# Polysketch attention and a rational activation on one Trainium2 core: two coefficients of the activation joined by accumulating transfers

## The chip, the cores and the metric

The kernel runs on one core of one Trainium2 chip. The metric is the device time of one execution in microseconds (us). Three executions of the kernel before took 264.3, 264.67 and 264.9 us; the median is 264.67 us.

## The reference, cut to what matters

Attention with a sketched polynomial feature map gives 4352 tokens of 128 features. They pass through a two-layer network whose activation is a quotient of two polynomials with coefficients a[0..3] and b[0..1]:

```python
h = x @ w_in                       # 4352 x 128 times 128 x 2048
P = a[0] + a[1] * h + a[2] * h**2 + a[3] * h**3
Q = 1.0 + abs(b[0]) * abs(h) + abs(b[1]) * h**2
g = P / (Q + 1e-06)
return g @ w_out                   # 2048 x 128
```

The attention in front of it builds, for each of 4 batches, products of two sketches (8 x 8 = 64 features for each head), sums k-features times v over the sequence, and divides numerator by denominator for each token.

## The kernel before, in words

**Units.** The network is cut into 21 units (`UNITS`): a stretch of tokens (mostly 512) and a group of 128-wide slices of the 2048 hidden features (mostly 8). A full unit is a tile of 128 x 4096 bf16 values. Units 3 to 16 are full ones, in pairs that share their tokens; units 0 to 2 and 17 to 20 are smaller. For a full unit these steps run:

- `H` (`hidden`, L498): TensorE multiplies, in four parts of 1024 columns, into PSUM.
- `E` (`evac`, L504): ScalarE copies each part to `hh` in bf16.
- `U` (`d_abs`, L511): VectorE clears the sign bit, u = |h|.
- `W` (`d_w`, L519): VectorE makes w = |b1| u + |b0|. `Y` (`d_y`, L524): VectorE multiplies w by u, so that w is Q - 1.
- `L` and `X` (`a_ln` L547, `a_exp` L551): ScalarE takes r = exp(-ln(1 + 1e-6 + w)) in two halves of 2048 columns; this is 1/Q.
- `P` (`p`): g = a3 h + a2 in two halves, each on VectorE (`.d`, L529) or on ScalarE (`.a`, L532). `V` (`d_hp`, L542): VectorE multiplies g by h.
- `S` (`d_s`, L555): s = h r. `G` (`d_g`, L559): g = g s. Both are on VectorE.
- `Or`, `Os`, `Og` (`gather`, L571): TensorE adds up r, s and g against w_out scaled by a0, by a1 and by 1. `ST` (L588) turns the finished 512 tokens round, `OUT` stores them.

Units named in `TWO` leave the a1 term out of `Os`: a step `A` (`plus`, L538) has the GpSimd queue issue two transfers per unit that add a DRAM tensor of a1 values (`ones`, f32) onto g between `V` and `G`. Then g = (a3 h^2 + a2 h + a1) s, and the eight matmuls of `Os` fall away. Before, units 6, 9 and 12 do so.

**What sets the order.** Nothing is scheduled by the compiler: `ORDER` is a list written out in full, and each engine works through its own instructions in that order. `H6.2` is part 2 of step H of unit 6; `K` and `Q` steps are the attention of a batch's keys and of a cut of its queries, `F` and `I` loads, `Z` matmuls on an idle tile. Semaphores follow from the tiles that a step reads and writes. Pools set how far steps may run ahead: `u` has one buffer, `w` two, `g` four, `hh` three, `r` and `s` two. GpSimd's queue holds only the transfers of `A` once the set-up is over. SP's queue holds all loads, the attention's writes and repeated reads through DRAM (`dw`, `dr`), and the stores.

Of the kernel before, what the change touches and what calls it, by code (L numbers as in the profile page):

```python
# [35 lines left out]
I0 I11 I1 I2 K0.T0 SS0 Z10 K0.s0 K0.T1 K0.c0.a K0.T2 K0.f0 Q0.0.T Z2 K0.s1 Z2 Q0.0.sk I3 Z2 K0.p0 I8 F1.k I7 I9 I5
I4 I10 I6 K0.c1.a K0.f1 Q0.0.c.d Q0.0.f Q0.1.T K0.p1 K0.k1.d Q0.2.T K1.T0 K0.k0.a Q0.1.sk K1.T1 Q0.0.p Q0.2.sk
Q0.0.pl.a Q0.1.c.a Q0.2.c.a Q0.0.r K1.T2 Q0.0.x K1.s0 Q0.0.b K1.s1 K1.c0.a Q0.0.kk.a w4.a K1.c1.a AB0 w0.a Q0.3.T
w2.d K1.f0 Q0.1.f K1.f1 w5.d H0.0 E0.0 Q0.1.p Q0.3.sk H1.0 H2.0 Q0.1.pl.a w1.a w3.a E1.0 Q0.3.c.a U0.0 Q0.1.r W0.0
P0.0.d Y0.0 V0.0 Q0.1.x Q0.2.dw F1.q U1.0 Q1.0.T W1.0 Q1.1.T P1.0.d Y1.0 H2.1 Q1.0.sk L0.0 E2.0 X0.0 E2.1 Q1.0.c.a  # L40
Q1.2.T S0.0 V1.0 U2.0 G0.0 P2.0.a F1.v K1.p0 K1.p1 Q0.1.b Or0.0 Os0.0 Og0.0 K1.k1.a K1.k0.a F2.k Q0.2.dr Q0.2.f
Q0.3.dw Q1.0.dw F2.q L1.0 Q0.1.kk.a Q0.2.p Q0.2.pl.a K2.T0 W2.0 K2.T1 Q0.2.r K2.T2 Q0.2.x Q1.1.sk Q1.1.c.a X1.0
K2.s0 Q0.2.b K2.s1 Q0.2.kk.a K2.c0.a Y2.0 H3.0 L2.0 K2.c1.a E3.0 S1.0 V2.0 K2.f0 G1.0 Q0.3.dr X2.0 Q1.1.dw H3.1
Q1.2.sk H3.2 E3.1 H3.3 Q1.0.dr Q2.0.T K2.f1 Q0.3.f S2.0 Q2.1.T G2.0 Q2.0.sk Q2.2.T E3.2 Q1.2.c.a E3.3 P3.0.a H4.0
Q0.3.p E4.0 Q0.3.pl.a Q2.0.c.a P3.1.a H4.1 U3.0 Q1.0.f W3.0 Q0.3.r Y3.0 Q1.0.p Q2.1.sk H4.2 Q1.0.pl.a E4.1 Q1.0.r
Q0.3.x Q1.0.x L3.0 P4.0.d V3.0 H4.3 Q0.3.b Os1.0 Q1.0.b Or1.0 Os2.0 E4.2 E4.3 F3.k Q1.1.dr Q1.1.f Q1.2.dw F3.q
Q2.1.c.a Q0.3.kk.a Q1.0.kk.a Q2.0.dw AW0 F2.v Q1.2.dr Q2.1.dw X3.0 Q2.0.dr Og1.0 H5.0 Q1.1.p Or2.0 L3.1 E5.0 X3.1
U4.0 P4.1.d W4.0 V4.0 Y4.0 H5.1 E5.1 Q1.1.pl.a H5.2 K2.p0 H5.3 S3.0 Q1.1.r P5.0.d G3.0 Q1.1.x Q3.0.T Q1.2.f L4.0
E5.2 X4.0 E5.3 K2.p1 Og2.0 ST2 U5.0 K2.k1.a K3.T0 W5.0 Q2.2.sk H6.0 K2.k0.a P5.1.a E6.0 L4.1 H6.1 Or3.0 Or3.1
Q1.1.b Q2.2.c.a E6.1 X4.1 Q1.1.kk.a Q3.0.sk H6.2 H6.3 Q1.2.p V5.0 Y5.0 L5.0 S4.0 P6.0.d Q2.0.f G4.0 Q2.1.dr E6.2  # L50
H7.0 X5.0 E6.3 L5.1 Q2.0.p Q2.0.pl.a Q1.2.pl.a Or4.1 H7.1 Or4.0 U6.0 Q3.1.T Q2.0.r Q1.2.r K3.T1 W6.0 K3.T2 Q2.1.f
E7.0 X5.1 P6.1.a Q2.2.dw E7.1 Q3.0.c.a Q3.0.dw OUT2 Y6.0 V6.0 Q2.0.x Os3.0 Og4.0 H7.2 L6.0 Q2.2.dr A6.0 F3.v X6.0
E7.2 L6.1 H7.3 E7.3 Os4.0 Og3.0 H8.0 S5.0 Q3.2.T Q1.2.x H8.1 Q1.2.b G5.0 K3.s0 P7.0.a E8.0 X6.1 E8.1 Q1.2.kk.a
Q2.0.b H8.2 U7.0 ST4 W7.0 P7.1.d Y7.0 K3.c0.a E8.2 S6.0 P8.0.d K3.f0 L7.0 Or5.0 H8.3 E8.3 P8.1.a Q2.0.kk.a Or5.1
Q2.1.p Q2.1.pl.a K3.s1 U8.0 V7.0 Q2.1.r W8.0 Q3.0.dr Q2.2.f K3.c1.a Y8.0 K3.f1 G6.0 Og5.0 Q3.1.sk H9.0 Os5.0 H9.1
X7.0 L7.1 E9.0 Q3.1.c.a X7.1 Q2.1.x Q3.1.dw L8.0 E9.1 V8.0 S7.0 H9.2 Or6.1 Or6.0 H9.3 E9.2 X8.0 E9.3 Q2.1.b H10.0
L8.1 Q2.1.kk.a Q2.2.p Og6.0 E10.0 Q2.2.pl.a X8.1 U9.0 G7.0 Q2.2.r W9.0 ST6 P9.0.a Q2.2.x Y9.0 H10.1 K3.p0 Or7.0
H10.2 E10.1 P9.1.a Or7.1 H10.3 K3.p1 E10.2 L9.0 E10.3 S8.0 V9.0 Q3.0.f U10.0 P10.0.d Q3.2.sk H11.0 X9.0 K3.k1.a
Q3.2.c.a H11.1 E11.0 L9.1 E11.1 K3.k0.a H11.2 Os7.0 G8.0 W10.0 P10.1.d Y10.0 E11.2 X9.1 H11.3 E11.3 L10.0 Og7.0
A9.0 Q3.2.dw Q3.1.dr Or8.0 Or8.1 V10.0 S9.0 U11.0 P11.0.a Q3.0.p Q3.0.pl.a X10.0 H12.0 Q2.2.b Os8.0 H12.1 Og8.0  # L60
E12.0 L10.1 Q2.2.kk.a X10.1 E12.1 OUT4 Q3.2.dr G9.0 Q3.1.f Q3.0.r W11.0 Q3.0.x Y11.0 S10.0 ST8 P11.1.a Q3.0.b
H12.2 Q3.0.kk.a E12.2 L11.0 OUT6 P12.0.d G10.0 V11.0 H12.3 E12.3 U12.0 Or9.0 Or9.1 X11.0 H13.0 E13.0 L11.1 H13.1
Q3.1.p E13.1 Q3.1.pl.a Og9.0 H13.2 H13.3 Or10.0 Or10.1 X11.1 E13.2 Q3.2.f W12.0 P12.1.d Q3.1.r Y12.0 L12.0 E13.3
P13.0.d S11.0 Q3.1.x U13.0 G11.0 W13.0 V12.0 X12.0 H14.0 Q3.1.b Q3.1.kk.a E14.0 P13.1.a H14.1 E14.1 L12.1 H14.2
Og10.0 E14.2 X12.1 H14.3 E14.3 Os10.0 Q3.2.p Y13.0 V13.0 ST10 H15.0 Or11.0 Or11.1 OUT8 A12.0 L13.0 U14.0 S12.0
P14.0.a Q3.2.pl.a X13.0 E15.0 L13.1 P14.1.d W14.0 Og11.0 H15.1 Os11.0 H15.2 E15.1 X13.1 V14.0 Y14.0 P15.0.d S13.0
G12.0 Q3.2.r E15.2 L14.0 Or12.0 H15.3 Or12.1 E15.3 U15.0 P15.1.d W15.0 Q3.2.x X14.0 H16.0 E16.0 L14.1 H16.1 Og12.0
E16.1 ST12 Y15.0 H16.2 Or13.0 Q3.2.b H16.3 X14.1 Or13.1 Or14.1 E16.2 Q3.2.kk.a L15.0 G13.0 S14.0 E16.3 U16.0.d
G14.0 W16.0.d V15.0 Y16.0 OUT12 OUT10 H17.0 Os13.0 H17.1 X15.0 E17.0 L15.1 P16.0.a E17.1 X15.1 Og14.0 H17.2 H17.3
Or14.0 Og13.0 P16.1.d E17.2 L16.0 E17.3 S15.0 V16.0 U17.0.d P17.0.d W17.0.d H18.0 H18.1 Os14.0 X16.0 E18.0 L16.1  # L70
E18.1 X16.1 P17.1.a ST14 Y17.0 G15.0 U18.0.d L17.0 W18.0.a P18.0.d S16.0 Y18.0 G16.0 H19.0 Or15.0 Or15.1 Os15.0
Or16.1 Or16.0 Os16.0 Og15.0 Og16.0 X17.0 E19.0 L17.1 U19.0.a X17.1 V17.0 W19.0.d ST16 S17.0 L18.0 P19.0.a Or17.0
H20.0 Os17.0 Or17.1 E20.0 X18.0 Y19.0 G17.0 V18.0 S18.0 Og17.0 OUT14 OUT16 U20.0.a L19.0 X19.0 W20.0.d ST17 Y20.0
V19.0 S19.0 OUT17 G18.0 P20.0.a L20.0 G19.0 V20.0 Z4 Or18.0 X20.0 Os18.0 Or19.0 Os19.0 Og18.0 S20.0 Og19.0 Or20.0
Os20.0 G20.0 Og20.0 ST20 OUT20
"""


# [1 line left out]
def kernel(  # L80
# [440 lines left out]

    def d_y(i, k):
        c = span(i, "Y", k)
        nc.vector.tensor_mul(out=at(i, "w", *c), in0=at(i, "w", *c), in1=at(i, "u", *c))  # L524
# [172 lines left out]
```

## Time and profile before

| | |
|---|---|
| median of three executions | 264.67 us (264.3 to 264.9) |
| profiled execution | 264.51 us |
| its span, first to last instruction | 262.7 us |
| granted TensorE clock | 1.000 |
| VectorE busy | 251.7 us in 234 instructions |
| ScalarE busy | 241.1 us in 230 instructions |
| TensorE busy | 253.7 us |
| GpSimd busy | 9.6 us in 31 instructions |

The span is 1.8 us shorter than the execution's own time. A busy time is the union of an engine's instructions; instructions of one engine overlap in the records by some 0.1 us at their ends, so the pace of a row (from one start to the next) is a little under its duration. TensorE's ends are modelled, so its busy time says less than the other two.

### The profile page before, as it was taken

The page shows a single profiled execution, that of the slowest core. Times are in us where ns is not written, and L with a number is a line of the kernel's source. Part 1 is how long each engine was busy: PE and PEld are TensorE (multiplying, and loading weights), DVE is VectorE, ACT ScalarE, POOL GpSimd, SP SyncE. Part 2 cuts the span into 40 slices and gives each one's busy share as a digit, 9 for nine tenths or more (in the row PEclk, how much of TensorE's full clock was granted, in tenths as well). Part 3 has the DMA queues.
Part 4 walks back from the last instruction along what each step waited for, and adds up shares of the span by engine and source line. Part 5 has one row for each costly group of instructions (what it writes and reads, how often), then busy time and mean ns, then how long its engine had stood idle before and what let it go on. Part 6 is the DMA issues. An engine that isn't in the chain of part 4 may idle for free.

```text
span 262.7 us, 3774 instructions
## 1 busy us (share of the span) xinstructions
PE 253.7 (97%) x1445; PEld 146.8 (56%) x1445; DVE 251.7 (96%) x234; ACT 241.1 (92%) x230; POOL 9.6 (4%) x31
## 2 busy tenths in 40 slices
...
GB/s 174 277 304 266 157 209 192 279 217 148 55 14 2 20 112 177 145 71 0 0 2 117 193 164 44 0 0 9 128 26 0 66 14 0 2 40 0 40 22 20
DMA packets 31888, 24.35 MB, mean 93 GB/s; under 512 B 19072, under 2 KB 26880, under 8 KB 31872
## 3 DMA queue, kind: packets, MB, share of 16 engines
...
q0 software_dynamic: 864, 3.15, 9.7%
q8 instruction: 11, 0.18, 0.3%
...
## 4 chain that ended last, share of the span: by engine, by line
PE 66%; DVE 13%; ACT 12%; issue 5%; DMA 2%; SPq 0%; DVEq 0%
PE h_ps L498 35%; PE out_ps L571 16%; PE att_ps L413 5%; ACT r L551 4%; ACT ln L547 4%; DVE s L555 3%; PE att_ps L319 3%; DVE g L559 2%; PE att_ps L291 2%; ACT hh L504 2%; DVE g L542 2%; DVE w L524 2%; PE att_ps L354 2%; DMA k_sb<-in_k_dram 2%; PE att_ps L441 1%
## 5 line engine op out<-in xcount | busy, mean ns | idle before, releaser
L498 PE MATMUL h_ps<-xT,w_in_sb 128*128 128x512 f32 (+1 forms) x320 | 126.4, 533 | 0.0
L498 PEld LDWEIGHTS h_ps<-xT,w_in_sb 128*128 128x128 f32 x320 | 58.7, 190 | 42.8 <-issue 34.3
L504 ACT CAST hh<-h_ps 128x1024 bf16<-128x1024 f32 x68 | 71.6, 1054 | 1.5 <-PE h_ps L498 1.3
L547 ACT ACTIVATE ln<-w 128x2048 f32<-128x2048 bf16 (+1 forms) x36 | 67.6, 1877 | 0.3 <-DVE w L524 0.2
L551 ACT ACTIVATE r<-ln 128x2048 bf16<-128x2048 f32 (+1 forms) x36 | 67.6, 1878 | 0.1
L571 PEld LDWEIGHTS <-w_out 128*128 128x128 bf16 x408 | 39.7, 98 | 47.6 <-issue 14.9
L555 DVE TENSOR_TENSOR s<-hh,r 128x4096 bf16<-128x4096 bf16 (+2 forms) x21 | 39.3, 1873 | 0.5 <-ACT r L551 0.3
L542 DVE TENSOR_TENSOR g<-g,hh 128x4096 bf16<-128x4096 bf16 (+2 forms) x21 | 39.4, 1874 | 0.0
L559 DVE TENSOR_TENSOR g<-g,s 128x4096 bf16<-128x4096 bf16 (+2 forms) x21 | 39.2, 1872 | 0.0
L524 DVE TENSOR_TENSOR w<-w,u 128x4096 bf16<-128x4096 bf16 (+2 forms) x21 | 39.2, 1866 | 0.0
L532 ACT ACTIVATE g<-hh,a_sb 128x2048 bf16<-128x2048 bf16 (+1 forms) x17 | 34.7, 2040 | 0.1
L571 PE MATMUL out_ps<-r,w_out 128*128 128x512 bf16 (+1 forms) x144 | 31.6, 356 | 1.3 <-DVE out_sb L588 1.3
L571 PE MATMUL out_ps<-g,w_out 128*128 128x512 bf16 (+1 forms) x144 | 30.4, 355 | 0.0
L571 PE MATMUL out_ps<-s,w_out 128*128 128x512 bf16 (+1 forms) x120 | 24.9, 350 | 1.9 <-DVE s L555 1.9
L519 DVE TENSOR_SCALAR w<-u,b_abs 128x4096 bf16<-128x4096 bf16 (+2 forms) x20 | 22.6, 1132 | 0.0
L511 DVE TENSOR_SCALAR u<-hh 128x4096 uint16<-128x4096 uint16 (+2 forms) x19 | 20.4, 1075 | 0.1
L413 PEld LDWEIGHTS att_ps<-kvz,a_all 128*118 128x118 f32 (+2 forms) x144 | 17.1, 186 | 4.4 <-issue 3.5
L413 PE MATMUL att_ps<-kvz,a_all 128*118 128x66 f32 (+2 forms) x144 | 16.9, 266 | 0.0
L529 DVE TENSOR_SCALAR g<-hh,a_sb 128x2048 bf16<-128x2048 bf16 (+1 forms) x19 | 14.6, 767 | 0.0
L538 POOL DMA_DIRECT2D g<-ones x6 | 6.3, 1337 | 166.9 <-DVE x_tok L435 81.0
L319 PEld LDWEIGHTS att_ps<-v_sb,k_p 128*64 128x64 f32 (+1 forms) x288 | 9.0, 138 | 3.5 <-issue 3.0
L285 DVE STREAM_TRANSPOSE kT<-k_sb 128x512 f32<-128x512 f32 (+2 forms) x12 | 6.2, 529 | 3.8 <-DMA k_sb<-in_k_dram 3.8
...
## 6 DMA issues: line engine op xcount, KB each, us to landing
...
```

Source lines behind the costliest of these rows:

```text
L413: nc.tensor.matmul(self.nd[:self.tl, o:o + 2 * KW], lhsT=self.group(t, c), rhs=kvz[self.b % 2][:, c, :], start=True, stop=True)
L498: nc.tensor.matmul(t[:, (x - part * m) * tl:(x - part * m + 1) * tl], lhsT=w_in_sb[:, (f0 + x) * 128:(f0 + x + 1) * 128], rhs=xT[:, p:p + ...
L504: nc.scalar.copy(out=at(i, "hh", c, ce), in_=live[i]["h", part][:, :ce - c])
L519: nc.vector.tensor_scalar(out=at(i, "w", *c), in0=at(i, "u", *c), scalar1=ab1, scalar2=ab0, op0=AX.mult, op1=AX.add)
L524: nc.vector.tensor_mul(out=at(i, "w", *c), in0=at(i, "w", *c), in1=at(i, "u", *c))
L532: nc.scalar.activation(out=at(i, "g", *c), in_=at(i, "hh", *c), func=ACT.Identity, scale=a3, bias=a2)
L542: nc.vector.tensor_mul(out=at(i, "g", *c), in0=at(i, "g", *c), in1=at(i, "hh", *c))
L547: nc.scalar.activation(out=t[:, :ce - c], in_=at(i, "w", c, ce), func=ACT.Ln, bias=1.0 + 1e-6)
L551: nc.scalar.activation(out=at(i, "r", c, ce), in_=live[i]["ln", k][:, :ce - c], func=ACT.Exp, scale=-1.0)
L555: nc.vector.tensor_mul(out=at(i, "s", *c), in0=at(i, "hh", *c), in1=at(i, "r", *c))
L559: nc.vector.tensor_mul(out=at(i, "g", *c), in0=at(i, "g", *c), in1=at(i, "s", *c))
L571: nc.tensor.matmul(outs[t0][:, :tl], lhsT=w, rhs=z, start=first and j == 0, stop=left[t0] == 0)
```

## The change

`TWO` grows from three units to six, 4, 6, 8, 10, 12 and 14. A new list `SQ` names units 5, 7, 9, 11, 13 and 15. In these the product of step `Y` is no longer made. A new step `D` (`square`) has ScalarE write w = (sqrt(|b1|) h)^2 from `hh`, in two halves. Step `W` scales u by |b0| in place. A new step `M` (`join`) has GpSimd's queue issue two transfers that add u onto w. Then `L` goes on from w as before. sqrt(|b1|) is made once, by a logarithm and an exponential on ScalarE.

In `ORDER` most halves of `P` that ScalarE made go to VectorE: 6 instead of 17 stay on ScalarE. Some small copies and sums change their engine too, and the rest of the list is written anew, with each engine's steps shifted by some places. In the changed kernel the lines are: U L516, W L527 (in place: L522), D L532, M L538, Y L542, P L547 on VectorE and L550 on ScalarE, A L556, V L560, L L565, X L569, S L573, G L577, gather L589.

```diff
-TWO = (6, 9, 12)
+TWO = (4, 6, 8, 10, 12, 14)
+SQ = (5, 7, 9, 11, 13, 15)
...
+    root1 = consts.tile([128, 1], FP, name="root1")
+    tiny = consts.tile([128, 1], FP, name="tiny")
+    nc.gpsimd.memset(tiny, 1e-30)
...
     def d_w(i, k, eng="d"):
         c = span(i, "W", k)
+        if i in SQ:
+            nc.vector.tensor_scalar(out=at(i, "u", *c), in0=at(i, "u", *c), scalar1=ab0, scalar2=None, op0=AX.mult)
+            return
...
+    def square(i, k):
+        c = span(i, "D", k)
+        nc.scalar.activation(out=at(i, "w", *c), in_=at(i, "hh", *c), func=ACT.Square, scale=root1)
+
+    def join(i, k):
+
+        c = span(i, "Y", k)
+        for x in range(c[0], c[1], 2048):
+            nc.gpsimd.dma_start(out=at(i, "w", x, x + 2048), in_=at(i, "u", x, x + 2048), accum_op=AX.add)
...
         nc.scalar.activation(out=b_abs, in_=b_sb, func=ACT.Abs)
+        if SQ:
+            nc.scalar.activation(out=root1, in_=ab1, func=ACT.Ln, bias=tiny)
+            nc.scalar.activation(out=root1, in_=root1, func=ACT.Exp, scale=0.5)
```

The part of the new list around the last `SQ` unit, which the prediction speaks of, is this (line breaks set here):

```
H14.2 Or11.0 Or11.1 H14.3 E14.2 X12.1 A12.0 S12.0 E14.3 L13.0 H15.0 Q3.2.p P14.1.d U14.0 V14.0 W14.0 E15.0 X13.0
H15.1 Os11.0 Or12.1 H15.2 E15.1 L13.1 E15.2 D15.0 H15.3 E15.3 X13.1 D15.1 Y14.0 G12.0 U15.0 H16.0 Or12.0 Og12.0
Og11.0 H16.1 L14.0 W15.0 S13.0 ST12 P15.0.d Q3.2.pl.a G13.0 P15.1.d Q3.2.r V15.0 Q3.2.x X14.0 E16.0 L14.1 E16.1
X14.1 Or13.0 Or13.1 H16.2 Or14.0 H16.3 Q3.2.b P16.0.d E16.2 Q3.2.kk.a E16.3 A14.0 M15.0 S14.0 L15.0 OUT10 OUT12
U16.0.d G14.0
```

More of the change, by code (lines that the diff above doesn't have):

```diff
@@ L35 @@
 ORDER = """
[L36 to L75, printed above, removed]
+I0 I11 I1 I2 K0.T0 SS0 Z10 K0.s0 K0.T1 K0.c0.a K0.T2 K0.f0 Q0.0.T Z2 K0.s1 K0.c1.a K0.f1 Q0.1.T Z2 Q0.0.sk I3 Z2
@@ new lines @@
+K0.p0 Q0.1.sk K0.p1 I7 F1.k I8 I9 I4 Q0.0.c.d Q0.1.c.a Q0.0.f Q0.2.T Q0.3.T Q0.2.sk Q0.1.f K0.k1.d K1.T0 K0.k0.a
+Q0.2.c.a Z2 Q0.0.p Q0.3.sk K1.T1 Q0.0.pl.a Q0.0.r I5 F1.q Q0.0.x Q0.1.p w2.d Q0.1.pl.d Q0.1.r Q0.1.x w4.d K1.T2
+Q0.3.c.a Q0.0.b Q0.2.dw I10 Q0.3.dw K1.s0 AB0 w0.a Q0.0.kk.a H0.0 K1.c0.a E0.0 K1.f0 Q1.0.T K1.s1 Q0.1.b H1.0
+Q1.0.sk I6 H2.0 Q1.1.T P0.0.a U0.0 W0.0 w5.d Y0.0 K1.c1.d Q1.2.T K1.f1 w1.a Q0.1.kk.a E1.0 w3.a P1.0.d U1.0 L0.0
+Q1.0.c.a X0.0 E2.0 V0.0 V1.0 W1.0 S0.0 Y1.0 H2.1 F1.v K1.p0 K1.p1 Or0.0 E2.1 L1.0 K1.k0.a Q0.2.dr F2.k Q1.0.dw
@@ new lines @@
+F2.q Q0.2.f Q0.2.p Q0.2.pl.a K1.k1.a G0.0 U2.0 Q0.2.r Q0.2.x Og0.0 Q1.1.sk Os0.0 Q0.2.b Q1.2.sk Q1.1.c.a X1.0
+K2.T0 Q0.3.dr K2.s0 W2.0 K2.T1 S1.0 Y2.0 Q2.0.T G1.0 K2.T2 Q2.1.T Q0.3.f Q0.2.kk.a Q1.2.c.a P2.0.a K2.c0.a H3.0
+E3.0 L2.0 H3.1 K2.s1 Q2.0.sk H3.2 K2.c1.a E3.1 V2.0 K2.f0 X2.0 Q2.2.T K2.f1 S2.0 Q1.1.dw Q1.0.dr H3.3 Q0.3.p E3.2
+E3.3 Q2.0.c.a Q0.3.pl.a P3.0.a Q1.0.f U3.0 Q0.3.r W3.0 Q0.3.x Q1.1.dr Q1.2.dw F3.q Q2.0.dw F3.k AW0 F2.v H4.0
+Q1.0.p H4.1 E4.0 Q1.0.pl.a P3.1.a E4.1 Q1.0.r Y3.0 Q1.0.x Q1.1.f P4.0.d V3.0 G2.0 Q2.1.sk Q0.3.b H4.2 L3.0 Q1.0.b
@@ new lines @@
+E4.2 Q0.3.kk.a Q2.1.c.a Q1.0.kk.a Or1.0 H4.3 Q2.2.sk H5.0 E4.3 Q1.2.dr Q2.0.dr Q2.1.dw P4.1.d U4.0 V4.0 W4.0
+Q3.0.T Y4.0 X3.0 E5.0 Q2.2.c.a L3.1 Os1.0 Os2.0 H5.1 H5.2 E5.1 X3.1 E5.2 H5.3 Or2.0 Q1.1.p Og1.0 H6.0 K2.p0 K2.p1
+Og2.0 E5.3 D5.0 Q1.1.pl.a D5.1 S3.0 U5.0 P5.0.d W5.0 P5.1.d Q1.1.r Q1.2.f Q1.1.x V5.0 ST2 E6.0 L4.0 Q2.2.dw
+K2.k0.a X4.0 H6.1 E6.1 K2.k1.a Q1.2.p Q1.2.pl.a G3.0 H6.2 Q3.0.sk H6.3 Or3.0 Q1.1.b L4.1 Q3.0.c.a X4.1 E6.2 Q3.1.T
+P6.0.d Q1.2.r K3.T0 Q1.2.x Q2.0.f S4.0 K3.T1 Q1.1.kk.a Q1.2.b K3.s0 Q3.1.sk H7.0 Or3.1 E6.3 A4.0 H7.1 M5.0 K3.c0.a
@@ new lines @@
+Q3.1.c.a Q1.2.kk.a L5.0 E7.0 X5.0 Q2.0.p H7.2 Q2.1.dr Q3.0.dw Q2.2.dr OUT2 E7.1 L5.1 E7.2 K3.f0 G4.0 U6.0 P6.1.d
+W6.0 Q2.0.pl.d Q2.1.f Y6.0 D7.0 H7.3 Og3.0 Os3.0 Or4.0 Or4.1 Q2.1.p Q3.2.T K3.T2 K3.s1 Q2.0.r Q2.2.f E7.3 U7.0
+X5.1 Q2.0.x W7.0 Q3.0.dr Q3.1.dw D7.1 L6.0 K3.c1.a P7.0.d S5.0 P7.1.d Q3.0.f V6.0 X6.0 H8.0 E8.0 Q2.1.pl.a Q2.1.r
+G5.0 H8.1 L6.1 Og4.0 Q2.0.b H8.2 E8.1 X6.1 E8.2 Q2.0.kk.a H8.3 E8.3 M7.0 L7.0 ST4 P8.0.d S6.0 Q2.1.x U8.0 P8.1.d
+W8.0 V8.0 Y8.0 K3.f1 Or5.0 H9.0 Or5.1 H9.1 E9.0 X7.0 E9.1 L7.1 H9.2 H9.3 Os5.0 Og5.0 Or6.0 F3.v E9.2 E9.3 D9.0
@@ new lines @@
+X7.1 D9.1 L8.0 H10.0 Q2.1.b Or6.1 Q2.1.kk.a H10.1 Q2.2.p K3.p0 K3.p1 X8.0 Q3.1.dr OUT4 A6.0 U9.0 P9.0.d W9.0 V7.0
+S7.0 G6.0 E10.0 L8.1 Og6.0 H10.2 Q2.2.pl.a K3.k1.a E10.1 X8.1 E10.2 K3.k0.a H10.3 M9.0 E10.3 L9.0 P9.1.d Q3.1.f
+V9.0 P10.0.d ST6 S8.0 P10.1.d U10.0 V10.0 Q2.2.r W10.0 Q2.2.x Or7.0 H11.0 E11.0 Or7.1 H11.1 A8.0 X9.0 E11.1 L9.1
+Or8.0 H11.2 Or8.1 H11.3 Y10.0 G7.0 E11.2 Q3.0.p Q3.0.pl.d H12.0 Os7.0 Q2.2.b Og7.0 D11.0 E11.3 X9.1 U11.0 Q3.0.r
+W11.0 G8.0 S9.0 P11.0.d H12.1 Q3.1.p Og8.0 G9.0 P11.1.d Q3.0.x Q3.1.pl.d ST8 V11.0 D11.1 L10.0 Q2.2.kk.a X10.0
@@ new lines @@
+E12.0 L10.1 H12.2 Q3.0.b E12.1 X10.1 A10.0 H12.3 E12.2 Q3.0.kk.a M11.0 E12.3 L11.0 Or9.0 H13.0 Or9.1 Q3.2.sk H13.1
+Q3.1.r S10.0 U12.0 P12.0.d Q3.2.c.d W12.0 P12.1.d G10.0 Y12.0 E13.0 X11.0 E13.1 L11.1 H13.2 E13.2 Og9.0 H13.3
+H14.0 Or10.0 Os9.0 P13.0.d Q3.1.x Q3.1.b Or10.1 Og10.0 D13.0 E13.3 H14.1 U13.0 OUT6 Q3.2.dw OUT8 Q3.2.dr X11.1
+P13.1.d W13.0 S11.0 D13.1 L12.0 Q3.1.kk.a E14.0 X12.0 E14.1 V12.0 ST10 G11.0 P14.0.d V13.0 Q3.2.f M13.0 L12.1
+H14.2 Or11.0 Or11.1 H14.3 E14.2 X12.1 A12.0 S12.0 E14.3 L13.0 H15.0 Q3.2.p P14.1.d U14.0 V14.0 W14.0 E15.0 X13.0
@@ new lines @@
+H15.1 Os11.0 Or12.1 H15.2 E15.1 L13.1 E15.2 D15.0 H15.3 E15.3 X13.1 D15.1 Y14.0 G12.0 U15.0 H16.0 Or12.0 Og12.0
+Og11.0 H16.1 L14.0 W15.0 S13.0 ST12 P15.0.d Q3.2.pl.a G13.0 P15.1.d Q3.2.r V15.0 Q3.2.x X14.0 E16.0 L14.1 E16.1
+X14.1 Or13.0 Or13.1 H16.2 Or14.0 H16.3 Q3.2.b P16.0.d E16.2 Q3.2.kk.a E16.3 A14.0 M15.0 S14.0 L15.0 OUT10 OUT12
+U16.0.d G14.0 P16.1.d W16.0.d V16.0 Y16.0 H17.0 E17.0 X15.0 H17.1 H17.2 E17.1 L15.1 E17.2 X15.1 Or14.1 H17.3
+Os13.0 Og14.0 Og13.0 E17.3 L16.0 S15.0 U17.0.d X16.0 H18.0 L16.1 E18.0 ST14 Or15.0 H18.1 X16.1 E18.1 W17.0.d
@@ L76 @@
+P17.0.d Y17.0 G15.0 U18.0.d L17.0 W18.0.a S16.0 P17.1.d G16.0 Or16.0 Os15.0 H19.0 Or15.1 Or16.1 Og15.0 Os16.0
+Og16.0 Y18.0 P18.0.d V17.0 X17.0 E19.0 L17.1 U19.0.a ST16 W19.0.d X17.1 S17.0 Y19.0 G17.0 Or17.0 H20.0 Or17.1
+Os17.0 P19.0.a L18.0 E20.0 X18.0 U20.0.d V18.0 S18.0 W20.0.a L19.0 X19.0 P20.0.a OUT14 OUT16 Z1 Og17.0 ST17 G18.0
+Y20.0 S19.0 V19.0 V20.0 G19.0 L20.0 OUT17 Z4 Or18.0 X20.0 Or19.0 Os18.0 Og18.0 Os19.0 Or20.0 Og19.0 S20.0 Os20.0
+G20.0 Og20.0 ST20 OUT20
 """
```

2 lines of the change are left out of this document (1 added, 1 removed).

## The prediction, on record before the changed kernel ran

> **What bounds the kernel now.** I read the busy times by stretch first, then the groups, then the order of time around the transfers that the kernel already makes. In the stretches (start:end and length; then busy time and count of TensorE, its weight load, VectorE, ScalarE, GpSimd; clock, DMA share, GB/s):
>
> ```profile
> 39.41:52.54 13.13, 13.13 (x59) 7.14 (x58) 13.13 (x16) 11.64 (x14) 0.00 (x0) 1.00 0.86 235
> 144.48:157.62 13.14, 13.14 (x62) 7.10 (x60) 13.14 (x10) 13.14 (x12) 0.00 (x0) 1.00 0.87 179
> 197.03:210.16 13.13, 13.13 (x45) 5.93 (x44) 13.13 (x11) 13.13 (x12) 0.00 (x0) 1.00 0.22 33
> 236.43:249.56 13.13, 10.49 (x64) 6.77 (x64) 12.81 (x9) 13.10 (x10) 0.00 (x0) 1.00 0.14 20
> 249.56:262.70 13.13, 8.98 (x120) 7.47 (x117) 8.99 (x14) 7.21 (x8) 0.00 (x0) 1.00 0.11 21
> ```
>
> From about 52 us to 249 us VectorE and ScalarE are busy in every microsecond, and TensorE nearly so until 236. So no single engine is to be relieved; all three must lose work before the end moves, and ScalarE is the one to look at: its idle time (262.7 - 241.1 = 21.6 us) lies in the first 52 us (15.2, by the four stretches up to there) and after its last big instruction (5.9). The clock is 1.00 throughout and takes no part.
>
> The prices, with the instruction's form, count, busy time and mean ns:
>
> ```profile
> L551 ACT ACTIVATE r<-ln 128x2048 bf16<-128x2048 f32 x32 | 63.3, 1979 | 0.0
> L532 ACT ACTIVATE g<-hh,a_sb 128x2048 bf16<-128x2048 bf16 x15 | 32.2, 2148 | 0.1
> L637 ACT ACTIVATE w_out<-ln,a_sb 128x1024 bf16<-128x1024 f32 x3 | 3.3, 1147 | 0.0
> L524 DVE TENSOR_TENSOR w<-w,u 128x4096 bf16<-128x4096 bf16 x15 | 34.0, 2270 | 0.0
> L529 DVE TENSOR_SCALAR g<-hh,a_sb 128x2048 bf16<-128x2048 bf16 x17 | 13.5, 795 | 0.0
> ```
>
> In the order of time, what counts is the step from one start to the next: exp and ln 1.81 us, P on ScalarE 1.99, an evacuation 0.90; on VectorE a full product 2.20, U 1.13, W 1.26, a half of P 0.72. Eight output matmuls take 1.73 us on TensorE (0.216 each).
>
> And the transfers that the kernel has, first in order of time (start, length), VectorE and then GpSimd:
>
> ```profile
> 132.88 2.28 DVE L542 TENSOR_TENSOR g<-g,hh 128x4096 bf16<-128x4096 bf16 x1
> 135.08 0.95 DVE L398 TENSOR_TENSOR a_all<-a_all,b_all 128x768 f32<-128x768 f32 x1
> 135.95 1.35 DVE L511 TENSOR_SCALAR u<-hh 128x4096 uint16<-128x4096 uint16 x1
> ```
>
> ```profile
> 135.68 2.60 POOL L538 DMA_DIRECT2D g<-ones  x2 [42.40 <-PE att_ps L354]
> ```
>
> then from the view of line L538, and the queue's packets, MB and share:
>
> ```profile
> DMA to landing us min/median/max: 7.1/9.1/11.7
> ```
>
> ```profile
> q0 software_dynamic: 864, 3.15, 9.7%
> ```
>
> GpSimd issues 0.5 us after the product it depends on has ended, both issues take 1.7 to 2.6 us, and the data has landed 7.1 us (the best) to 11.7 us (the worst) after its issue. The six transfers took 9.7% of 16 engines' span, 25.5 us or 4.25 us each with all engines on it.
>
> **The change, part by part.**
>
> *TensorE.* Three more units without Os: 24 matmuls x 0.216 = -5.2 us. Three more idle matmuls: +0.65. Net -4.5.
>
> *VectorE.* Six products Y go: 6 x 2.20 = -13.2. Twelve halves of P come: 12 x 0.72 = +8.6. W in place is the same form as before: 0. By the instruction lists one small P half and one small W less, one small U, four denominators, two sketch copies and one weight cast more: -0.45 - 0.44 + 0.34 + 0.6 + 0.4 + 0.6 = +1.05. Net -3.5. Against that, beside the issue at 135.68 the U took a step of 1.28 us instead of 1.13; nine more pairs of issues give 0 to +1.4. I take -3.
>
> *ScalarE.* Twelve halves of P leave: 12 x 1.99 = -23.9. Twelve squares come. No row shows a square; it reads bf16, writes bf16 and has one coefficient per partition. Without such an operand 2048 columns take 1.81 us, with two 1.99, and the weight scaling with one is 0.10 us longer than the bare cast of its size (1147 against 1048 ns). So 1.81 to 1.99; I take 1.90, +22.8. The two small steps for the root, a small P and a small W come, a small U, four denominators, a weight cast and two small copies go: +0.3 + 1.1 + 1.1 - 0.95 - 0.5 - 0.95 - 0.4 = -0.3. Net -1.4 (bounds -2.5 to -0.3).
>
> So **ScalarE loses least, and it has no idle time between 52 us and 250 us to give back**. If no new wait appears, its 1.4 us is what the end gains. VectorE's 3 us and TensorE's 4.5 us turn into slack, and into shorter waits only where ScalarE still idles, before 52 us.
>
> *The new wait.* L of an SQ unit waited for Y, 2.2 us of VectorE behind W. Now it waits for M, issued when W and the second square are done. Behind L in ScalarE's queue stand the evacuations, for which TensorE waits, and X, for which S and the rest of VectorE wait. How long may M take? In unit 15, VectorE does G12, U15 and W15 after Y14: 2.20 + 1.13 + 1.26 = 4.6 us. ScalarE does L14.0, X14.0, L14.1, X14.1, four evacuations and two small steps between the start of L14.0, which needs Y14, and L15.0: 4 x 1.81 + 4 x 0.90 + 0.4 = 11.2. That leaves 6.6 us after W, plus whatever ScalarE runs behind VectorE: in the trace L starts 0.4 to 1.8 us after its Y has ended. The other five units give 6.6 to 7.7 in the same way. So **7 to 8.4 us are covered**, for the first of the two transfers alone (L.0 needs only the first half). The old transfers' best case would fill that: 0.5 + 7.1 = 7.6. But they read 1 MB of f32 from DRAM; M reads 0.5 MB of bf16 from SBUF, and both also read and write the 0.5 MB they add to. If bytes read count, M takes two thirds of 4.25 us, 2.8; if elements count, 4.25; if source bytes, 2.1. I take 2.8, by the row of the same kind of transfer; the first half then lands 0.5 + 7.1 - 1.4 = 6.2 us after W, and the wait is covered. At 4.25 it is on the edge.
>
> U of the next unit waits too, since `u` has one buffer and M reads it. Behind W15 stand S13, ST12, P15.0, G13, P15.1, V15, two short steps, P16.0 and S14, 12.2 us, against 0.5 + 11.7 at worst: covered. G waits for A behind at least 16 us of VectorE work: covered. The A pair of unit 14 is issued at V14, 8 us before M15, on the same queue, and takes 8.5 us of data time: M15 may start some 2 us late, and 0 to 1 us of ScalarE is lost there. What the early idle time gives back is of the same size, 0 to 1 us. I let these two cancel.
>
> *DMA as a whole.* Six transfers more of the old kind (25 us) and twelve new ones (34 us at 2.8) come onto DMA engines that were busy 0.05 to 0.2 of the time in many stretches but 0.86 to 0.99 in others, where the attention's repeats run. The pair at 135.68 landed after 9.8 us (median of its two) while repeats ran beside it, so sharing costs one or two microseconds, not ten. SP's queue gets no transfer that it did not have.
>
> [...]
>
> **The sum.** The profiled execution took 264.5 us (span 262.7 + 1.8), 0.2 below the median of 264.67. 264.5 - 1.4 = 263.1; from the median 263.3. I say 263.2.
>
> **The rivals.**
>
> - *The sum of u and w lands late* (slower). Place: L.0 of the six SQ units. It decides from about 7.5 us after W. If M is as slow as the old median (0.5 + 9.1 = 9.6), each unit waits up to 2 us; VectorE then gets ahead, so that the next unit is allowed more, and I count half: 6 x 1.0 = 6, so 263.2 + 6 = 269. With 0.5 us each: 266. [...] For it: the cover is thin and DMA gets busier. Against it: half the source bytes, and issues that ran beside products.
> - *VectorE's saving is what counts* (faster still). ScalarE's 4 us of idle time between 13 and 52 us is filled, and squares take 1.81: 264.5 - 3.0 = 261.5. For it: VectorE and TensorE bring the early units sooner. Against it: the early steps' own work hardly changes.
> - *Nothing moves.* Squares cost as P, and small stalls take the rest: 264.3.
> - *It does not do what it says.* The square needs another function table, 1.28 us per load (L154). The instruction list holds one table load, as before, so I give it nothing.
>
> **How the numbers follow.** Forecast, 262.2 to 264.1: 0.40. Faster still: 0.18. Within 0.2% (0.5 us, about what a measurement of this kernel can tell from no change): 0.14. Late sums: 0.28. So faster 0.58, same 0.14, slower 0.28. The range goes from 260.8 (ScalarE's -2.5 and another 1.2 us of early idle time) up to 267.2, into the late sums; about one in ten is left out on each side.
>
> **What would show it.** Right: ScalarE still without idle time from 52 us on, the square at 1.9 us a step, idle time of some microseconds newly on VectorE and TensorE, M's transfers landing within 6 to 8 us. Wrong: ScalarE idle ahead of ln (L565) released by a DMA, or VectorE idle ahead of U (L516), which would put the late sums on record; GpSimd's issues above 3 us for a pair; attention products on VectorE waiting for their repeats.

## The result, and the profile after

The changed kernel took 266.03 us (median of 20 executions, 264.51 to 267.04) against 264.67 us before (20 executions, 264.04 to 265.29). The ratio is 1.0046, 95% interval [1.0029, 1.0062]: slower, by about 1.2 us (1.4 by the medians), where 1.5 us less was forecast. The profiled execution is the fastest of them, 264.51 us with a span of 262.7 us, the same two numbers as before. So the trace holds the change at its best, and has to be read by stages.

Busy times and the granted clock by slice, from the page of the changed kernel:

```profile
PE 250.6 (95%) x1410; PEld 144.8 (55%) x1424; DVE 249.2 (95%) x246; ACT 239.8 (91%) x226; POOL 24.7 (9%) x50
...
PEclk9999999999999999999999999999999999999799
```

ScalarE's busy time fell from 241.1 to 239.8 us, by 1.3 (forecast 1.4). In slice 38 (243.0 to 249.6 us) the clock is not whole (a 7), which it was throughout before (a 9 in every slice, 1.000 on average). The view by stretches (columns as in the prediction) shows where idle time now lies:

```profile
13.13:26.27 13.14, 11.87 (x81) 10.01 (x78) 12.07 (x26) 9.71 (x19) 0.00 (x0) 1.00 0.86 229
39.41:52.54 13.13, 13.13 (x63) 7.59 (x60) 12.98 (x16) 12.94 (x14) 0.00 (x0) 1.00 0.88 241
144.48:157.62 13.14, 12.81 (x55) 6.64 (x55) 12.65 (x14) 13.14 (x10) 1.75 (x2) 1.00 0.79 129
197.03:210.16 13.13, 12.01 (x41) 4.99 (x41) 12.95 (x12) 13.13 (x11) 1.76 (x2) 1.00 0.97 156
236.43:249.56 13.13, 10.46 (x56) 6.79 (x55) 13.12 (x12) 12.13 (x10) 0.00 (x0) 0.87 0.13 20
249.56:262.70 13.14, 9.23 (x124) 7.99 (x122) 8.26 (x12) 7.47 (x8) 0.00 (x0) 1.00 0.11 22
```

In the rows from 144.48 and 197.03 only ScalarE is still full; TensorE has gaps, as the change wants. In the row from 236.43 the clock is 0.87 and ScalarE idles for 1 us. And in the row from 13.13, all engines and the DMA were busier before:

```profile
13.13:26.27 13.14, 13.14 (x92) 11.14 (x90) 12.73 (x25) 10.84 (x19) 0.00 (x0) 1.00 0.97 285
```

The new operations, by the groups of the changed kernel, and the data's landing from the view of line L538:

```profile
L532 ACT ACTIVATE w<-hh,root 128x2048 bf16<-128x2048 bf16 x12 | 24.8, 2072 | 0.0
```

```profile
DMA to landing us min/median/max: 4.6/6.4/10.3
```

**Where the time went, by stage.** I divide the execution by the starts of five ScalarE steps: K0.c0.a (its first step of the attention), E0.0, E4.0, X17.0 and X20.0 (its last big step). All in us; the last column is the sum, from K0.c0.a to X20.0. The other kernels are told of below.

| kernel | K0.c0.a to E0.0 | E0.0 to E4.0 | E4.0 to X17.0 | X17.0 to X20.0 | sum |
|---|---|---|---|---|---|
| before | 12.97 | 25.44 | 192.52 | 18.41 | 249.34 |
| after | 13.62 | 26.78 | 189.96 | 19.37 | 249.73 |
| again | 13.62 | 29.89 | 190.02 | 19.44 | 252.97 |
| h20_first | 13.62 | 26.72 | 190.03 | 18.34 | 248.71 |
| i6_early | 13.62 | 25.96 | 190.03 | 19.60 | 249.21 |
| both | 13.62 | 25.95 | 190.03 | 18.35 | 247.95 |
| both_two3 | 13.90 | 25.95 | 192.31 | 18.35 | 250.51 |
| before_two6 | 13.25 | 25.44 | 192.52 | 18.41 | 249.62 |
| before_i6_late | 13.09 | 26.63 | 192.58 | 18.44 | 250.74 |
| both_copy | 13.30 | 25.92 | 189.97 | 18.33 | 247.53 |

So the middle, where the squares and the transfers work, gained 2.5 us. The start and the end, where they do not, gave it all back. (The sums are differences of the starts as the profiles show them, so they can differ by 0.01 from the sum of a row.)

**The start.** Loads and writes on SP's queue in order of time (start, length, line, operation), before and then after:

```profile
10.20 2.00 SPq L176 DMA_DIRECT2D w_in_sb<-in_moe_w_in_dram  x1
15.45 1.31 SPq L380 DMA_DIRECT2D sk_d<-sk_sb  x2
16.86 0.53 SPq L134 DMA_DIRECT2D q_sb<-in_q_dram  x1
```

```profile
12.46 0.33 SPq L136 DMA_DIRECT2D q_sb<-in_q_dram  x1
13.87 1.39 SPq L385 DMA_DIRECT2D sk_d<-sk_sb  x2
15.30 0.59 SPq L188 DMA_DIRECT2D ln<-in_moe_w_out_dram  x1
15.99 1.17 SPq L385 DMA_DIRECT2D sk_d<-sk_sb  x2
17.21 0.58 SPq L178 DMA_DIRECT2D w_in_sb<-in_moe_w_in_dram  x1
```

The load of w_in's second half (step I6) was issued at 10.20 us before. In the new list it stands behind F1.q, which waits for a free q buffer, and behind two writes that wait for sketches. It goes out at 17.21, and TensorE waits for it ahead of H2.0. The wait differs from execution to execution: 0.80 us in the profile of after, and 0.94 to 1.54 in those of h20_first, no_plus, z_fill and no_join below, which have the load at the same late place. Here are TensorE's rows in the profiles of after, of no_join, and of the unchanged kernel run once more ("again", 268.49 us):

```profile
23.91 3.69 PE L503 MATMUL h_ps<-xT,w_in_sb 128*128 128x256 f32 x16 [0.80 <-DMA w_in_sb<-in_moe_w_in_dram]
```

```profile
25.35 3.69 PE L503 MATMUL h_ps<-xT,w_in_sb 128*128 128x256 f32 x16 [1.54 <-DMA w_in_sb<-in_moe_w_in_dram]
```

```profile
26.28 5.38 PE L503 MATMUL h_ps<-xT,w_in_sb 128*128 128x256 f32 x16 [2.42 <-DMA w_in_sb<-in_moe_w_in_dram]
```

The third row shows two losses: 2.42 us of waiting, and then 5.38 us for the same 16 matmuls that took 3.69, with a lowered clock (the page of again has a 7 in its fifth slice too, 26.7 to 33.3 us; the 1.69 us more are what 3.4 us at a clock of 0.5 would cost, by my estimate). This execution is a slow one, over 1.5% above the fastest of its kernel, so the account of the loss takes no size from it.

**The end.** TensorE's rows around H20.0 (the f32 row with 8 matmuls), before (with the gap that comes ahead of it) and after, the clock in the stretch 243.00 to 246.42 after, and ScalarE's next evacuation after:

```profile
237.78 1.89 PE L571 MATMUL out_ps<-s,w_out 128*128 128x512 bf16 x8 [1.89 <-DVE s L555]
...
244.41 1.05 PE L571 MATMUL out_ps<-r,w_out 128*128 128x256 bf16 x8 [1.28 <-DVE out_sb L588]
245.29 1.89 PE L498 MATMUL h_ps<-xT,w_in_sb 128*128 128x256 f32 x8
```

```profile
243.41 1.89 PE L589 MATMUL out_ps<-r,w_out 128*128 128x256 bf16 x8 [2.67 <-DVE out_sb L606]
245.09 2.55 PE L503 MATMUL h_ps<-xT,w_in_sb 128*128 128x256 f32 x8
```

```profile
243.00:246.42 3.42, 3.01 (x12) 2.32 (x13) 3.41 (x4) 3.42 (x3) 0.00 (x0) 0.50 0.49 77
```

```profile
247.68 1.01 ACT L509 CAST hh<-h_ps 128x1024 bf16<-128x1024 f32 x1 [1.00 <-PE h_ps L503]
```

TensorE now runs out of work for 2.67 us until ST16 (L606), which stands behind V17 on VectorE in both lists, has emptied a bank of out_ps. Before, it idled for 1.89 us ahead of unit 16's `s` sums and for 1.28 here. So it does not idle longer than before, but all at one place. The same eight `r` matmuls then take 1.89 instead of 1.05 us and H20.0 2.55 instead of 1.89, at a clock of 0.50 in the stretch shown, and ScalarE waits 1.00 us for E20.0.

### The profile page after: what moved, and what is told of

It reads as the page before. It is cut to its first block, busy times and chain, and to the rows that moved or that the text cites. A ratio compares the mean times of both kernels' runs of the same rounds, so it can differ in the third digit from the quotient of the medians.

```text
span 262.7 us, 3775 instructions
## 1 busy us (share of the span) xinstructions
PE 250.6 (95%) x1410; PEld 144.8 (55%) x1424; DVE 249.2 (95%) x246; ACT 239.8 (91%) x226; POOL 24.7 (9%) x50
## 4 chain that ended last, share of the span: by engine, by line
ACT 55%; PE 20%; issue 14%; DVE 6%; DMA 2%; SPq 0%; DVEq 0%; ACTq 0%
ACT hh L509 16%; ACT ln L565 15%; ACT r L569 14%; PE h_ps L503 8%; ACT w L532 7%; DMA w_in_sb<-in_moe_w_in_dram 2%; PE out_ps L199 2%; PE out_ps L589 2%; PE att_ps L324 2%; PE att_ps L418 2%; DVE w L542 1%; ACT xT L265 1%; PE att_ps L359 1%; DVE s L573 1%; PE h_ps L296 1%
## 5 line engine op out<-in xcount | busy, mean ns | idle before, releaser
L565 ACT ACTIVATE ln<-w 128x2048 f32<-128x2048 bf16 (+1 forms) x36 | 67.0, 1861 | 0.1
L569 ACT ACTIVATE r<-ln 128x2048 bf16<-128x2048 f32 (+1 forms) x36 | 66.8, 1856 | 0.1
L589 PEld LDWEIGHTS <-w_out 128*128 128x128 bf16 x384 | 37.5, 99 | 46.1 <-issue 14.0
L573 DVE TENSOR_TENSOR s<-hh,r 128x4096 bf16<-128x4096 bf16 (+2 forms) x21 | 39.3, 1873 | 0.5 <-ACT r L569 0.2
L577 DVE TENSOR_TENSOR g<-g,s 128x4096 bf16<-128x4096 bf16 (+2 forms) x21 | 39.2, 1867 | 0.0
L560 DVE TENSOR_TENSOR g<-g,hh 128x4096 bf16<-128x4096 bf16 (+2 forms) x21 | 39.2, 1874 | 0.0
L589 PE MATMUL out_ps<-r,w_out 128*128 128x512 bf16 (+1 forms) x141 | 33.1, 363 | 2.8 <-DVE out_sb L606 2.7
L589 PE MATMUL out_ps<-g,w_out 128*128 128x512 bf16 (+1 forms) x140 | 29.8, 355 | 0.5 <-DVE g L577 0.2
L542 DVE TENSOR_TENSOR w<-w,u 128x4096 bf16<-128x4096 bf16 (+2 forms) x15 | 25.6, 1708 | 0.0
L532 ACT ACTIVATE w<-hh,root 128x2048 bf16<-128x2048 bf16 x12 | 24.8, 2072 | 0.0
L547 DVE TENSOR_SCALAR g<-hh,a_sb 128x2048 bf16<-128x2048 bf16 (+1 forms) x30 | 23.8, 792 | 0.2 <-PE out_ps L589 0.2
L516 DVE TENSOR_SCALAR u<-hh 128x4096 uint16<-128x4096 uint16 (+2 forms) x20 | 20.9, 1046 | 1.5 <-ACT hh L509 1.4
L538 POOL DMA_DIRECT2D w<-u x12 | 10.5, 968 | 88.5 <-DVE u L522 48.9
L556 POOL DMA_DIRECT2D g<-ones x12 | 11.2, 1042 | 80.2 <-PE h_ps L503 50.4
L589 PE MATMUL out_ps<-s,w_out 128*128 128x512 bf16 (+1 forms) x91 | 18.2, 342 | 0.2
L527 DVE TENSOR_SCALAR w<-u,b_abs 128x4096 bf16<-128x4096 bf16 (+2 forms) x13 | 14.3, 1099 | 0.0
L403 DVE TENSOR_TENSOR a_all<-a_all,b_all 128x704 f32<-128x704 f32 (+3 forms) x11 | 9.5, 863 | 0.7 <-DMA b_all<-sk_d 0.7
```

The source lines that it names most:

```text
L532: nc.scalar.activation(out=at(i, "w", *c), in_=at(i, "hh", *c), func=ACT.Square, scale=root1)
L547: nc.vector.tensor_scalar(out=at(i, "g", *c), in0=at(i, "hh", *c), scalar1=a3, scalar2=a2, op0=AX.mult, op1=AX.add)
L560: nc.vector.tensor_mul(out=at(i, "g", *c), in0=at(i, "g", *c), in1=at(i, "hh", *c))
L565: nc.scalar.activation(out=t[:, :ce - c], in_=at(i, "w", c, ce), func=ACT.Ln, bias=1.0 + 1e-6)
L569: nc.scalar.activation(out=at(i, "r", c, ce), in_=live[i]["ln", k][:, :ce - c], func=ACT.Exp, scale=-1.0)
L573: nc.vector.tensor_mul(out=at(i, "s", *c), in0=at(i, "hh", *c), in1=at(i, "r", *c))
```

## The experiments

My theory after the two traces: the squares and sums do what was forecast, and the loss is two places of the new list, I6 on SP's queue and the TensorE gap ahead of Or17.0. The rival: the transfers (DMA load, late sums) cost the time somewhere.

**again**: the changed kernel, nothing edited.

> The changed kernel, unchanged. Its one profile so far is of its fastest execution (264.5 us), its median was 266.0 and its executions spread over 2.5 us, those of before over 1.3. Order theory: ScalarE does 1.3 us less work, and the new list gives it back in idle time (0.8 us more ahead of the first units, 1.0 us near the end behind a half-speed stretch of TensorE's clock); a profile of a longer execution shows more idle time on ScalarE at places of that kind. Transfer theory: a longer execution shows VectorE or ScalarE waiting for a landing (the sums, or the attention's repeats) somewhere between 60 and 210 us. Both expect 266.0 +- 0.6.

266.02 us (12 executions: ten from 263.95 to 267.17, two at 268.5), ratio 1.0034 [1.0009, 1.0059] to 264.76. The loss is there again, with a spread of 3.2 us in the ten, where all but one of 35 executions of the kernel before lie within 2.1 us; its profile is the one with the 2.42 us wait.

**no_join** and **no_plus**: the transfers of `M`, or those of `A`, left out.

```diff
-        for x in range(c[0], c[1], 2048):
-            nc.gpsimd.dma_start(out=at(i, "w", x, x + 2048), in_=at(i, "u", x, x + 2048), accum_op=AX.add)
+        return
```

> Leaves out the step M, so that u is not added and the denominators of six units lack their linear term; all other work stays. Order theory: ln never waited for M (in the profile it starts 3 to 8 us after the first half has landed), so 266.0, within 0.5. Transfer theory: 12 of the 24 transfers are gone, and with them their contention: 264.5 or less, and a narrower spread.

> Leaves out the step A, so that six units lack their a1 term; all other work stays. Order theory: 266.0, within 0.5. Transfer theory: these twelve read f32 from DRAM and keep the DMA engines busy 4 us each, more than M does; without them 264.5 or less and a narrower spread.

266.08 us, ratio 1.0051 [1.0026, 1.0076], and 266.57 us, 1.0053 [1.0024, 1.0081]. (The second lies just outside the 0.5 us of the order theory, on the side away from the transfer theory.) Taking the transfers away gives nothing back: E4.0 to X17.0 is 190.02 us in both. The rival falls.

**h20_first**: H20.0 goes ahead of Or17.0, so that TensorE has work while the bank is emptied.

```diff
-S17.0 Y19.0 G17.0 Or17.0 H20.0 Or17.1
+S17.0 Y19.0 G17.0 H20.0 Or17.0 Or17.1
```

> H20.0 is put ahead of Or17.0 in the list, so that TensorE has 1.7 us of work in its 2.7 us gap before unit 17's sums. Order theory: no half-speed stretch, E20.0 no longer 1.0 us late, 0.7 to 1.0 us less than the changed kernel. Transfer theory: what makes the long executions long lies earlier, so the executions spread as before over 2 us and the median falls by 0.5 at most.

264.74 us (263.81 to 267.57), ratio 1.0013 [0.9981, 1.0045]; X17.0 to X20.0 falls from 19.37 to 18.34 us. TensorE's rows:

```profile
240.96 1.89 PE L503 MATMUL h_ps<-xT,w_in_sb 128*128 128x256 f32 x8
243.79 1.92 PE L589 MATMUL out_ps<-r,w_out 128*128 128x256 bf16 x16 [0.94 <-DVE out_sb L606]
```

The gap is 0.94 us, and the clock has a 9 in every slice. The median is 1.3 us below that of the changed kernel, where 0.7 to 1.0 was expected. Nine executions lie at 263.8 to 264.8 us, with a granted clock of 0.997 to 1.000, and three at 267.0 to 267.6, with 0.994. One stretch of 3.4 us at half clock takes 0.5 x 3.4 / 264 = 0.006 off; so I take the three for executions that waited for I6 and lost clock as again did (2.42 us of waiting). That is an estimate: no trace of them is at hand.

**z_fill**: ten idle matmuls fill the gap; the order of the rest stays.

```diff
-G17.0 Or17.0 H20.0 Or17.1
+G17.0 Z10 Or17.0 H20.0 Or17.1
```

> The changed kernel with ten idle matmuls (2.2 us) ahead of Or17.0, in TensorE's 2.7 us gap; H20.0 stays where it is. Clock theory: what h20_first gained came from TensorE's clock staying at full speed, so this gains as much (median down by 0.7 to 1.3, no half-speed stretch at 243 us, E20.0 no longer waits). Rival, the place of H20.0: it gained because H20.0 came earlier; then this stays at 266.0, though the clock is full.

265.28 us, ratio 1.0022 [1.0000, 1.0044] to 264.9. X17.0 to X20.0 is 18.35 us at a granted clock of 1.000, as in h20_first (18.34 us, 0.998) and not as in after (19.37 us, 0.994), though Or17.0 still runs ahead of H20.0. So at the end it is the half-speed clock that costs the time, and not the place of H20.0 behind Or17.0. (Its profile also has a late load of k, and K0.c0.a to E0.0 takes 14.86 us.)

**i6_early**: I6 goes back ahead of F1.q.

```diff
-Q0.0.r I5 F1.q Q0.0.x
+Q0.0.r I5 I6 F1.q Q0.0.x
...
-Q1.0.sk I6 H2.0
+Q1.0.sk H2.0
```

> The changed kernel with I6, the load of the second half of w_in, put back right behind I5 on SP's queue (before the change it was issued at 10.2 us; in the changed list, behind a load that waits for a buffer and two writes, at 17.2 to 18.0). Load theory: in the changed kernel TensorE waited 0.8 to 2.4 us for this load ahead of H2.0, differently in each execution, and in one profile its clock fell to half there. With I6 early this wait is gone: 0.8 to 1.5 us less than the changed kernel (265.0 or less), with a narrower spread; the late half-speed stretch at 243 us stays. Rival, chance in the start: the spread and the median stay as they are (266.0).

264.03 us, ratio 0.9967 [0.9952, 0.9981] to 264.9; the executions now lie within 1 us (263.52 to 264.46). That is 2.0 us less than the changed kernel, more than the 0.8 to 1.5 expected. E0.0 to E4.0 is 25.96 us; in the six profiles with the late load it is 26.7 to 27.4, and 29.9 in again.

**both**: i6_early and h20_first together.

> I6 early and H20.0 ahead of Or17.0. If the two are the whole loss, this is what the change itself is worth once its list is mended: 264.7 - 1.4 = 263.3, by ScalarE's 1.3 us less work, between 262.8 and 263.8. If something else eats the gain as well, 264.2 or more.

263.65 us (262.88 to 264.26), ratio 0.9947 [0.9930, 0.9965] to 264.9: 1.3 us faster than before, which is what was forecast of the change itself. It is 2.4 us less than the changed kernel, where the two edits alone gave 2.0 and 1.3, so their gains overlap.

**both_no_sums**: both, with the transfers of `M` and of `A` left out.

> As both, and leaves out M and A: neither the linear term of six denominators nor the a1 term of six numerators is added. If the 24 transfers cost nothing by contention or issue, the same as both within 0.4 us. If they slow VectorE through GpSimd's issues, or the attention's repeats, 0.5 to 1.5 us less than both.

263.94 us, ratio 0.9961 [0.9948, 0.9974]. Against the 263.65 us of both, the twenty-four transfers cost nothing that can be measured.

**both_two3**: both, with units 4, 8 and 12 given their `Os` back, so that TensorE has its load of before while ScalarE and VectorE keep their savings.

```diff
-TWO = (4, 6, 8, 10, 12, 14)
+TWO = (6, 10, 14)
...
-G5.0 H8.1 L6.1 Og4.0
+G5.0 H8.1 L6.1 Os4.0 Og4.0
```

> Both edits of the list (load of w_in ahead of F1.q, H20.0 ahead of Or17.0) with the coefficient sums of units 4, 8 and 12 given back to TensorE: 24 output matmuls of 0.216 us more, +5.2 us of TensorE, 0 on ScalarE and VectorE. Theory (ScalarE sets the pace from 54 us to 236 us, TensorE's saving is slack there): 263.65 within 0.4 us. Rival (TensorE's saving is part of the gain, the middle is bound by all three): 264.5 to 266, with idle time of ScalarE ahead of evacuations of units 8 to 16.

266.28 us, ratio 1.0052 [1.0037, 1.0067] to 264.82. My theory missed and the rival held: the middle takes 192.31 us, 0.2 less than in the kernel before. TensorE is busy for 191.4 us of it, so that the place of the returned matmuls in the list can matter by the other 0.9 us at most. The chain of waits, of both and then of both_two3:

```profile
ACT 63%; PE 20%; issue 15%; DVE 1%; DVEq 0%; ACTq 0%
```

```profile
PE 60%; ACT 28%; issue 7%; DMA 2%; DVE 1%; SPq 0%; DVEq 0%
...
L509 ACT CAST hh<-h_ps 128x1024 bf16<-128x1024 f32 x68 | 69.7, 1030 | 4.2 <-PE h_ps L503 3.9
```

ScalarE waits 3.9 us for H (both: 2.1); 1.8 of it lies at evacuations of units 8, 12 and 13, in the stage where the matmuls came back and where both has none.

**before_two6**: the opposite half, the kernel before with only TensorE relieved.

```diff
-TWO = (6, 9, 12)
+TWO = (4, 6, 8, 9, 12, 14)
...
-U4.0 P4.1.d W4.0 V4.0 Y4.0
+U4.0 P4.1.d W4.0 V4.0 A4.0 Y4.0
...
-Os4.0 Og3.0
+Og3.0
```

Units 8 and 14 are edited in the same way.

> The kernel before with only TensorE's part of the change: units 4, 8 and 14 leave Os out as well and get the summing transfers (A behind V), 24 output matmuls of 0.216 us less, -5.2 us of TensorE, nothing else moved, no squares. Between the first evacuation of unit 4 and X17.0 the kernel before takes 192.5 us, with 191.5 of ScalarE and 192.2 of VectorE in it. Theory A (all three engines bound that stretch at the same level, so that TensorE's relief is worth only the small gaps of the other two): -0.2 to -1.0 us, 263.8 to 264.6. Theory B (TensorE alone was the bound, as the chain of waits of before with 66% on it says, and the change's gain in that stretch, 2.5 us, is TensorE's): -2 us or more, 262.8 or less.

The middle takes 192.52 us, to a hundredth what it took before: theory B falls, and even the small gaps that theory A allowed did not close. Yet the chain of waits changes wholly, before and then before_two6:

```profile
PE 66%; DVE 13%; ACT 12%; issue 5%; DMA 2%; SPq 0%; DVEq 0%
```

```profile
ACT 42%; PE 25%; DVE 19%; issue 10%; DMA 2%; SPq 0%; DVEq 0%; ACTq 0%
```

The median was 266.06 us against 264.74, ratio 1.0046 [1.0031, 1.0062]. Of this 1.3 us the profiled execution (265.55) shows 0.7 ahead of E0.0 (K0.c0.a starts 0.4 later, E0.0 another 0.3) and 0.4 outside the span; from E0.0 to X20.0 nothing differs. But it is not typical of the six: its granted clock is 0.997, and four of the others have 0.990 or 0.991, which is what one half-speed stretch of 3.4 us more would take off (0.006, worked out above). By my estimate its place is ahead of unit 16's `s` sums, where TensorE, with less to do, now idles for 2.56 us instead of 1.89; no trace of these four is at hand.

```profile
238.47 1.89 PE L571 MATMUL out_ps<-s,w_out 128*128 128x512 bf16 x8 [2.56 <-DVE s L555]
```

The gap ahead of Or17.0 is still 1.28 us here. So it is not TensorE's lighter load that made it 2.67 in the changed kernel, but the new list.

**before_i6_late**: the kernel before, with I6 behind a `dw` write and F1.q as in the new list.

```diff
-I4 I10 I6 K0.c1.a
+I4 I10 K0.c1.a
...
-H1.0 H2.0 Q0.1.pl.a
+H1.0 Q0.2.dw F1.q I6 H2.0 Q0.1.pl.a
```

> The kernel before with one thing of the new list: the load of the second half of w_in is issued behind a dw write and F1.q on SP's queue. Theory (the load's place is one part of the loss): TensorE waits 0.8 to 2.4 us for w_in ahead of H2.0, the median is 0.8 to 2 us slower than before, 265.5 to 266.9, with a wider spread of the executions. Rival (the late load only matters in the new kernel, where TensorE and VectorE arrive earlier): within 0.4 us of before.

265.74 us (264.76 to 269.6), ratio 1.0037 [1.0018, 1.0057] to 264.82: 0.9 us slower. The stage from E0.0 to E4.0 takes 26.63 us instead of 25.44, and every later stage is as before within 0.1 us. The place of I6 is harmful in either kernel.

**both_copy**: both, with the small copy of xT that H0.0 needs moved ahead of the root and of a weight scaling on ScalarE.

```diff
-K1.s0 AB0 w0.a Q0.0.kk.a H0.0 K1.c0.a E0.0
+K1.s0 Q0.0.kk.a H0.0 K1.c0.a AB0 w0.a E0.0
```

> Both edits of the list, and the small copy that H0.0 waits for (Q0.0.kk.a) goes ahead of the root's three small steps and of the 1.14 us weight scaling w0.a on ScalarE. Theory (that place of the copy is where the constant 0.65 us between K0.c0.a and E0.0 comes from): 12.5 to 13.0 us from K0.c0.a to E0.0 instead of 13.62, ScalarE's idle time ahead of E0.0 below 1 us instead of 1.92, median 262.8 to 263.3. Rival (the first evacuations are followed by steps that wait for VectorE anyway, so the time is given back before E4.0): 263.65 within 0.3 us, with more idle time of ScalarE between E0.0 and E4.0.

263.33 us, ratio 0.9929 [0.9912, 0.9947] to 265.37. K0.c0.a to E0.0 is 13.30 us instead of 13.62: half the 0.65 us, less than expected, since w0.a now runs until 19.64 and E0.0 follows right behind it. By the intervals it is not told apart from both, but it is the best of the runs.

## Why the prediction was wrong, point by point

- **ScalarE's sum was right**: 241.1 to 239.8 us busy. The squares took 1.89 to 1.90 us a step (forecast 1.90), and no idle time above 0.12 us appears between E4.0 and X17.0. VectorE's busy time fell by 2.5 us (forecast 3) and TensorE's, whose ends are modelled, by 3.1 (forecast 4.5).
- **The new wait was covered, as forecast.** The first half of `M` landed 5.1 to 7.1 us after W (forecast 6.2, cover 7 to 8.4), and L.0 started 5.0 to 8.5 us later still, 11.5 to 13.6 us after W: the cover was larger than I had worked out. The late sums, with their 0.28, did not come about; no_join (266.08 us against 266.03) and both_no_sums (263.94 against 263.65) show that the transfers cost nothing that can be measured. That the result, 266.03 us, is near the 266 of this rival, and so inside the stated range, is luck: none of it came about by that way.
- **GpSimd's issues ran beside VectorE's products**, as the prediction has it against the late sums. The twelve pairs took 1.7 to 2.3 us each (before: 1.74 to 2.60), and no issue waited for a product's end: the pair of M11 at 148.34 us took 1.76 us wholly beside two products (147.72 to 152.20 together). In the kernel before, the pair at 181.76 us took 1.74 us beside the product that starts at 181.17, and ended at 183.50, 0.1 us into the next.
- **The middle was mis-sized, to the good side.** "ScalarE loses least" and 1.4 us at the end: the middle gained 2.5. ScalarE's busy time there, by the starts and ends of its steps, fell from 191.5 to 189.6 us, since 0.9 us of its work went into the stage from E0.0 to E4.0, and 0.6 of its 1.0 us of small gaps closed as well. The statement "all three must lose work before the end moves" is borne out: TensorE's relief alone 192.52, the others' alone 192.31, all together 190.0, from 192.52. (ScalarE and VectorE were relieved only together, so which of the two is needed more stays open.)
- **The failing step** is the early stage: "SP's queue gets no transfer that it did not have", by which the late load was put at nothing, with "What the early idle time gives back is of the same size, 0 to 1 us", and, against a rival, "the early steps' own work hardly changes". I counted the queue's transfers and not their places. A load that had been there was moved behind three others that wait. The early stages gave nothing back and lost 2.0 us in the fastest execution (0.65 ahead of E0.0, 1.34 from E0.0 to E4.0), and more in others. Of the 1.34, 0.82 is I6 (26.78 against 25.96 in i6_early; 0.8 to 1.4 in the profiles of h20_first, no_plus, no_join and z_fill). The other 0.5 goes with work that the new list has there: in i6_early TensorE is busy for all of the 25.96 us (25.27 of 25.44 before), and ScalarE does 0.9 us more. No run takes that work out again. Of the 0.65, half is the place of one copy (both_copy); the rest is open.
- **The second part of it** is the end. "The clock is 1.00 throughout and takes no part" was read from the old list and carried over to the new one, and the sum had no term behind 236 us, though the stretch from there showed TensorE with 2.6 us idle. The new list turned two gaps of 1.89 and 1.28 us into one of 2.67, the clock fell to 0.50 for 3.4 us, and 1.0 us was lost.
- **Together**, from K0.c0.a to X20.0: +0.65 + 1.34 - 2.56 + 0.96 = +0.39 us in the fastest execution. The median's +1.36 probably holds more of the variable wait, since i6_early, which takes that wait away, lies 2.0 us lower and has a narrower spread. With the two places mended the same sum is +0.65 + 0.51 - 2.49 - 0.06 = -1.39, and both measured -1.25. That this meets the forecast of 1.4 is in part luck: ScalarE's work fell by the 1.3 us of the sum, but its idle time stayed the same overall only because 1.0 us more ahead of E0.0 met 0.4 less up to E4.0 and 0.65 less in the middle.
